# The first 128 tokens of expert 0 gathered from three batches and run through both layers before the gating of the last batch is done

## The chip, the cores and the metric

The kernel runs on one core of one Trainium2 chip. The metric is the device time of one execution in microseconds. A core has a matrix engine (TensorE: PE for its matmuls, PEld for its weight loads), three engines that work on vectors (VectorE or DVE, ScalarE or ACT, GpSimd or POOL) and SyncE (SP), which issues transfers. Each takes its instructions in order; they wait for one another by semaphores. Sixteen DMA engines carry the transfers, which SP, ACT and POOL issue.

## The reference

Causal attention with a decay bias, a mixture of eight experts with one expert per token, and a dense layer with a squared ReLU. Cut to what matters:

```python
# attention: B=4, H=8, S=576, D=64
cum = np.cumsum(np.maximum(s, 0.0), axis=-1)
scores = q @ k.T / np.sqrt(D) + np.minimum(-(cum[:, None] - cum[None, :]), 0.0)   # causal mask
attn_out = softmax(scores) @ v
x = attn_out.transpose(0, 2, 1, 3).reshape(2304, 512)
# mixture: E=8, D=512, F=1024
e_idx = np.argmax(x @ w_gate, axis=1)
gate_w = softmax(x @ w_gate)[arange, e_idx]
eom = sigmoid(x @ w_output_gate)
for e in range(8):
    mask = e_idx == e
    ye = np.maximum(x[mask] @ w1[e], 0.0) @ w2[e]
    out[mask] = gate_w[mask, None] * eom[mask, e, None] * ye
# dense: D=512, F=2048
r = np.maximum(out @ w_in, 0.0)
return (r * r) @ w_out
```

w_in and w_out reach the kernel as 64-bit words, which it converts itself.

## The kernel before

**Attention.** The 32 heads are worked on in 16 pairs, four pairs to a batch of 576 tokens. Scores come from L497, their softmax from DVE (L524) and ACT (L541), the probabilities are transposed on PE (L557) and multiplied by v (L595). The normalised result is transposed back (L633), multiplied by the gate weights (L635), and the token rows are written to a DRAM tensor `x_d`.

**Gating.** When a batch is through, a list of steps `s_lg` to `s_gq` finds each token's expert, its rank among the tokens of that expert (L781 to L785 on PE, L796 and L799 on DVE) and, by one-hot matrices `r` (L804) and small matmuls (`s_tb`, L814), adds to a table of 384 places per expert the number of the token that stands at each place (`tbl`, and `tbl_i` after the last batch, L823). Expert 0's first places are thus known before the last batch, the others only at the end. For the last batch the table is made in three chunks of 128 places, and as soon as a chunk is made, POOL gathers expert 0's rows of it from `x_d` by an indirect DMA (`gather`, L289). While PE has nothing to do in that stretch it runs matmuls on a constant that nobody reads: `warm` (L349, ten and seven) and `warm_h` (L1470, twelve).

**Expert stage.** Expert g has a fixed number of slots, 352 for expert 0, then 320, 304, 304, 288, 288, 272, 256. For precision every fp32 operand is split into a rounded high part and the rest ("hi" and "lo"), and each product takes three passes: hi x hi, lo x hi, hi x lo. The gathered rows are transposed by PE (`x_pe`, L1129), the high part is copied by ACT (`x_hi`, L1135), the low part is made by DVE (`x_lo`, L1140). The hidden layer has eight groups f = 0 to 7, each of 12 matmuls (`emit_h`, L1222), a ReLU on ACT (L1233) and the low part on DVE (L1234), both into one of three buffers of `h_p`; the output layer adds 12 matmuls for each f into four banks (`emit_y`, L1260). A group of h goes into one of four banks, z4 to z7, which the transposes use too (`bank_x`). So an expert takes 96 + 96 matmuls. The result goes to `yT_d`, each expert at the offset that it has in the list of tokens sorted by expert (`y_store`).

**What is loaded beside it.** A pair of halves of the next expert's weights ("a" for the hidden, "b" for the output layer) comes in eight loads of 0.5 MB (`w_load`, L232, on SP into three `stg` buffers and one `stx`), is rounded by ACT (`w_hi`, L241), and its rest is made by DVE (`w_lo`, L245). The 64-bit words of w_in and w_out are converted beside the experts by jobs on DVE, ACT and POOL (L1162 to L1191), whose places start at unit `cv0` and lie `cvp` units apart.

**Between gating and expert 0.** The steps of `perm_steps` count the tokens of every expert (`p_cnt`, L1359), make offsets and a table `tbl_p` of the token numbers of the experts 1 to 7 (DVE, L1364 to L1407), which every later gather needs, and find out whether some expert has more tokens than slots (`p_max`, L1412 on), in which case a loop behind the dense layer works on the rest. SP reads the offsets into registers (`load_regs`). The late gating steps `s_dl` to `s_gq` of batch 3 (`dl` and `zz` on POOL, the exponentials on ACT L855 and L857, the rest on DVE) make the factors by which outputs are multiplied.

**Order.** All of it is emitted as tasks `at(key, fn)`, sorted by key; each engine then works in the order in which its instructions were emitted. A unit of the key is one group f of the expert stage; `te` in the change is the key at which the last pair of heads starts.

Of the kernel before, what the change touches and what calls it, by code (L numbers as in the profile page):

```python
# [12 lines left out]
F32 = mybir.dt.float32  # L13
F32R = mybir.dt.float32r
# [59 lines left out]
    cvp=3.55,  # L74
    cv0=1.2,
# [12 lines left out]
def attention_moe_ffn_kernel(  # L88
# [72 lines left out]
    gap = const.tile([P, 1], F32, name="gap")  # L161
    slot_v = const.tile([1, 3, E], I32, name="slot_v")
# [117 lines left out]

    def gather(g, cs=None):
        if cs is None or cs[0] == 0:
            xr_t[g] = xr_p.tile([P, CH, DM], F32, tag="xr", name="xr")
        t = xr_t[g]
        for c, n in enumerate(rows_of(g)):
            if cs is not None and c not in cs:
                continue
            idx = tbl_i[0:n, c * E:c * E + 1] if g == 0 else tbl_p[0:n, c, g:g + 1]
            nc.gpsimd.indirect_dma_start(  # L289
                out=t[0:n, c, :], out_offset=None, in_=x_d[:, :],  # L290
                in_offset=bass.IndirectOffsetOnAxis(ap=idx, axis=0))
# [11 lines left out]
    with tc.manual_schedule():  # L303
        with ExitStack() as actx:
# [436 lines left out]
            def emit_gate(b, tg, gk):  # L741
# [46 lines left out]

                def s_oid():
# [11 lines left out]
                def s_r1(t, c0=0, c1=CH):  # L801
                    if t == 0 and c0 == 0:
# [70 lines left out]
                steps = [s_lg, s_mx, s_eq, s_cand, s_ix, s_oh, s_pr, s_oid, s_tm, s_rk]  # L873
                if last:
                    ahead = 2
                    for c in range(CH):
                        steps += [partial(s_r1, t, c, c + 1) for t in range(ahead if c else 0, NB)]
                        steps.append(partial(s_tb, c, c + 1))
                        if c + 1 < CH:
                            steps += [partial(s_r1, t, c + 1, c + 2) for t in range(ahead)]  # L880
                        steps += [partial(s_tbl, c, c + 1), partial(gather, 0, [c])]
                else:
                    steps += [partial(s_r1, t) for t in range(NB)] + [s_tb, s_tbl]
                rest = [s_cs, s_ca, s_dl, s_zs, s_pe, s_se, s_rr, s_gq]
                if last:
                    late_steps.extend(rest[2:])
                    steps += rest[0:2]
                else:
                    steps += rest
                for i, st_ in enumerate(steps):  # L890
                    at(tg + (0.001 * i if last else gk[i]), st_)
                if last:
                    at(tg + 0.0055, warm, K_["wm"][3])
                    at(tg + 0.0145, warm, K_["wm"][4])
# [228 lines left out]
        def x_pe(g, c, k0=0, k1=KD):  # L1123
            if c == 0:
                xt_t[g] = xt_p.tile([P, 2, KD, TT], F32R, tag="xt", name="xt")
# [7 lines left out]
        def x_hi(g, c, k0=0, k1=KD):  # L1133
            r = rows_of(g)[c]
            nc.scalar.copy(out=xt_t[g][:, 0, k0:k1, c * P:c * P + r], in_=xp_t[g, c, k0])  # L1135

        def x_lo(g, c, k0=0, k1=KD):
            r = rows_of(g)[c]
            xt = xt_t[g]
            nc.vector.tensor_tensor(  # L1140
                out=xt[:, 1, k0:k1, c * P:c * P + r], in0=xp_t.pop((g, c, k0)),
                in1=xt[:, 0, k0:k1, c * P:c * P + r].bitcast(F32), op=ALU.subtract)
# [71 lines left out]
        def emit_h(g, e, f, fl):  # L1214
            n = sum(rows_of(g))
# [12 lines left out]
        def emit_hv(g, f):  # L1228
            n = sum(rows_of(g))
# [17 lines left out]
        def emit_y(g, e, f, fl, nf, f0=0):  # L1247
# [5 lines left out]
            if g < E:  # L1253
                n = CAPS[g]
# [48 lines left out]
        def emit_yv(g):  # L1303
            ysb = ysb_t[g] = y_p.tile([P, 4, TT], F32, tag="ysb", name="ysb", bufs=1)
            if g < E:
                n = CAPS[g]
# [13 lines left out]
        def y_store(g):  # L1320
            ysb = ysb_t.pop(g)
            if g < E:
                n = CAPS[g]
                dst = yT_d.rearrange("(k p) n -> p k n", p=P)
                nc.sync.dma_start(
                    out=dst[:, :, 0:n] if g == 0 else dst[:, :, ds(reg_o[g], n)], in_=ysb[:, :, 0:n])
# [27 lines left out]
        def perm_steps():  # L1354
# [54 lines left out]
            def p_max():  # L1409
                f = [cnt_f[:, i:i + 1] for i in range(4)]  # L1410
                ov = gt2("ov", [E], 1)
                nc.vector.tensor_tensor(out=ov, in0=R["sv"][:, 2], in1=caps, op=ALU.is_gt)  # L1412
# [54 lines left out]
        def warm_h(n):  # L1467
            wt = bank_x()
            for _ in range(n):
                nc.tensor.matmul(  # L1470
                    wt, lhsT=onesb, rhs=onesb.unsqueeze(1).to_broadcast([P, 512 // P, P]), start=True, stop=True)
# [8 lines left out]
        at(-1.1, warm_h, K_["wm"][5])  # L1480
        for c in range(CH):
            x_trans(0, c, -1.0 + 0.1 * c)
            at(-1.0 + 0.1 * c + 0.0015, warm_h, K_["wm"][6 + c])
        at(0.3, gather, 1)
# [5 lines left out]
        for g in range(E):  # L1490
# [11 lines left out]
            for i, job in enumerate(hj):  # L1502
# [3 lines left out]
                w_job(job, max(ta - K_["wld"], -0.7), ta + K_['wh'], ta + K_['wl'])  # L1506
# [184 lines left out]
```

## Time and profile before

| | |
|---|---|
| time, median of 3 runs | 894.81 us (894.42 to 896.83) |
| time of the profiled execution | 893.0 us |
| its span, first to last instruction | 890.9 us |
| mean granted clock of TensorE | 0.992 |
| busy, share of the span | PE 96%, DVE 58%, ACT 50%, POOL 29% |
| moved by DMA | 121.26 MB, 136 GB/s on average |

A busy share is the time in which an engine works, as a part of the span. The granted clock is given as a part of 2.4 GHz; 0.5 is the lower level of 1.2 GHz. In rows of a timeline the first number is the start in microseconds, the second the time from the start of the row's first instruction to the end of its last, and the number in square brackets the idle time before it and what ended it. The start of the next row on the same engine, less this start, is the row's spacing; matmuls are pipelined, so a row's time is longer than its spacing.

### The profile page before, as it was taken

To read this page: it belongs to the slowest core of one execution; us is meant where nothing else is said; L and a number is where in the kernel's file an instruction comes from. 1 tells how busy PE (TensorE), PEld (TensorE's weight loads), DVE (VectorE), ACT (ScalarE), POOL (GpSimd) and SP (SyncE) were. 2 spreads that over 40 slices of the span, in tenths; PEclk is the share of its full clock that TensorE was granted. 3 is DMA by queue.
4 is the path that set the end of the run, shared out by engine and by line. 5 is a ranking of instruction groups with operands and counts; after the bars stand their busy time and mean duration, and the time that the engine had idled before them with its cause. 6 is when DMAs were issued, how large, how long until landed. Compare 5 with 4: busy or idle time off the path is not lost.

```text
span 890.9 us, 15118 instructions
## 1 busy us (share of the span) xinstructions
PE 854.2 (96%) x5397; PEld 750.0 (84%) x5397; DVE 520.6 (58%) x1180; ACT 448.2 (50%) x997; POOL 261.5 (29%) x299
## 2 busy tenths in 40 slices
PE   7999998899989999999999999999999999999993
PEld 5777776667579999999999888899999999999993
DVE  8777867677666776778766566655333333322221
ACT  6687778788435555655565445444233322322221
POOL 4433144532225455665301232323011011001001
PEclk9999999999999999999999999999999999999997
DMA  6687788886267888988976333221202100000001
GB/s 158 150 192 185 179 198 204 208 189 152 60 207 241 244 232 263 271 263 249 295 228 173 87 119 94 92 86 61 70 36 71 37 37 36 1 1 36 1 0 39
DMA packets 89013, 121.26 MB, mean 136 GB/s; under 512 B 33505, under 2 KB 59105, under 8 KB 88034
## 3 DMA queue, kind: packets, MB, share of 16 engines
q1 hardware_dynamic: 82674, 105.34, 43.7%
q0 software_dynamic: 3664, 9.62, 3.3%
q10 hardware_dynamic: 2592, 5.24, 1.7%
q8 instruction: 45, 0.74, 0.4%
q14 instruction: 38, 0.31, 0.1%
HBM read 80.50 MB, written 23.17 MB: 116 GB/s over the span
## 4 chain that ended last, share of the span: by engine, by line
PE 34%; issue 31%; POOL 9%; ACT 7%; DMA 6%; DVE 6%; SPq 3%; POOLq 0%; ACTq 0%; DVEq 0%
PE z L1260 11%; PE z L1222 11%; PE t L595 3%; PE s L497 3%; POOL cvm L1191 3%; PE t L557 2%; POOL cvm L1190 2%; POOL out_dram L1329 2%; ACT p L541 2%; DMA w_in_d<-cvm 1%; PE z L1129 1%; DVE cvs L1184 1%; DMA xr<-x_d,tbl_p 1%; SPq L448 1%; DMA sta<-aug_d 1%
## 5 line engine op out<-in xcount | busy, mean ns | idle before, releaser
L1222 PE MATMUL z<-xt,w 128*128 128x384 f32 (+6 forms) x1920 | 334.9, 323 | 3.1 <-DVE r L1240 3.0
L1222 PEld LDWEIGHTS z<-xt,w 128*128 128x128 f32 x1920 | 311.6, 188 | 14.1 <-DVE r L1240 6.2
L1269 PE MATMUL z<-w,h 128*128 128x512 f32 x864 | 215.0, 393 | 0.0
L1269 PEld LDWEIGHTS z<-w,h 128*128 128x128 f32 x864 | 160.8, 188 | 29.3
L1240 DVE SCALAR_TENSOR_TENSOR r<-z,r 128x384 f32<-128x384 f32 x96 | 53.3, 555 | 132.4 <-ACT r L1239 131.9
L1260 PE MATMUL z<-h,w 128*128 128x304 f32 (+5 forms) x768 | 115.0, 299 | 0.0
L1239 ACT ACTIVATE r<-z 128x384 f32<-128x384 f32 x96 | 46.8, 488 | 129.2 <-PE z L1222 127.4
L1260 PEld LDWEIGHTS z<-h,w 128*128 128x128 f32 x768 | 108.0, 188 | 0.0
L1190 POOL TENSOR_TENSOR cvm<-cvm,cva 128x512 f32<-128x512 f32 x32 | 43.6, 1361 | 208.5 <-DVE cva L1186 135.7
L1242 ACT CAST h<-r 128x384 fp32r<-128x384 f32 x96 | 49.3, 513 | 85.6 <-DVE r L1240 85.6
L1243 DVE TENSOR_TENSOR h<-r,h 128x384 fp32r<-128x384 f32 x96 | 58.3, 608 | 55.7 <-ACT h L1242 55.7
L1329 POOL DMA_INDIRECT out_dram<-ysb,tok_m x18 | 17.4, 968 | 238.6 <-ACT ysb L1316 176.4
L541 ACT ACTIVATE p<-p,nm 128x128 f32<-128x128 f32 (+3 forms) x144 | 84.4, 591 | 3.9 <-DVE nm L524 3.8
L524 DVE CUSTOM_DVE_ANT_0 p<-s,mask 128x128 f32<-128x128 f32 (+3 forms) x128 | 59.8, 486 | 33.3 <-PE s L497 32.5
L557 PE MATMUL t<-ident,p 128*128 128x128 f32 x400 | 67.4, 281 | 2.2 <-ACT pt L576 0.7
L245 DVE TENSOR_TENSOR w<-stg,w 128x1024 fp32r<-128x1024 f32 x49 | 67.7, 1381 | 0.5 <-ACT w L241 0.4
L557 PEld LDWEIGHTS t<-ident,p 128*128 128x128 f32 x400 | 45.2, 141 | 15.8 <-ACT p L541 8.0
L497 PE MATMUL s<-sta 68*128 68x192 f32 (+7 forms) x204 | 49.8, 340 | 7.9 <-DMA sta<-aug_d 6.7
L1234 DVE SCALAR_TENSOR_TENSOR h<-z,h 128x304 fp32r<-128x304 f32 (+5 forms) x64 | 29.6, 462 | 47.3 <-ACT h L1233 47.1
L241 ACT CAST w<-stg 128x1024 fp32r<-128x1024 f32 x49 | 51.2, 1045 | 8.8 <-DMA stg<-in_moe_w_dram 5.6
L1191 POOL TENSOR_TENSOR cvm<-cvs,cvm 128x512 f32<-128x512 f32 x32 | 54.0, 1686 | 2.5
L595 PE MATMUL t<-pt,v 128*64 128x320 f32 (+4 forms) x448 | 53.1, 368 | 0.0
(223 smaller groups left out, 1016.1 us busy)
## 6 DMA issues: line engine op xcount, KB each, us to landing
stg<-in_moe_w_dram SPq DMA_DIRECT2D x42, 512.0 KB
cv<-in_moe_w_out_dram SPq DMA_DIRECT2D x16, 512.0 KB
stb<-sta SPq DMA_DIRECT2D x14, 576.0 KB
stx<-in_moe_w_dram SPq DMA_DIRECT2D x14, 512.0 KB
cv<-in_moe_w_in_dram SPq DMA_DIRECT2D x14, 512.0 KB
xr<-yT_d SPq DMA_DIRECT2D x8, 768.0 KB
q<-in_q_dram SPq DMA_DIRECT2D x16, 256.0 KB
k<-in_k_dram SPq DMA_DIRECT2D x16, 256.0 KB
```

The costliest lines, as they stand in the source:

```text
L245: nc.vector.tensor_tensor(out=lo, in0=raw.pop(job), in1=hi.bitcast(F32), op=ALU.subtract)
L497: nc.tensor.matmul(ps[0:mw, d0:d0 + nn], lhsT=ql[r, m0:m0 + mw], rhs=kl[r, c0:c0 + nn], start=(i == 0 and (tail or n == 0)), stop=(done an ...
L524: nc.vector.tensor_tensor_reduce(out=dst, in0=src, in1=msk, scale=-1.0, scalar=3.0e38, op0=ALU.add, op1=ALU.min, accum_out=nm[:, c:c + 1])
L541: nc.scalar.activation(out=pt[:, cs], in_=pt[:, cs], func=AF.Exp, scale=-1.0, bias=nm[:, c:c + 1], accum_out=rs[:, r:r + 1])
L557: nc.tensor.transpose(tp[:, i * P:(i + 1) * P], pt[:, j0:j0 + P], ident)
L595: nc.tensor.matmul(o[64 * hd:64 * hd + 64, c0:n], lhsT=vt[r0:P, jb, hd, :], rhs=pt[r0:P, hd, jb, c0:n], start=(jb == 0), stop=(jb == last))
L1190: nc.gpsimd.tensor_tensor(out=m, in0=m, in1=a.bitcast(F32), op=ALU.mult)
L1191: nc.gpsimd.tensor_tensor(out=m, in0=sq, in1=m, op=ALU.add)
L1222: nc.tensor.matmul(ps[:, 0:n], lhsT=wa[:, zw, kk, fl * P:(fl + 1) * P], rhs=xt[:, zx, kk, 0:n], start=(i == 0), stop=(i == 3 * KD - 1))
L1243: nc.vector.tensor_tensor(out=ht[:, 1, 0:n], in0=gg, in1=ht[:, 0, 0:n].bitcast(F32), op=ALU.subtract)
L1260: nc.tensor.matmul(y_acc[g][d][:, 0:n], lhsT=wb[:, zw, fl, d * P:(d + 1) * P], rhs=ht[:, zh, 0:n], start=(f == 0 and i == 0), stop=(f == n ...
L1269: nc.tensor.matmul(acc, lhsT=ht[:, zh, c * P:(c + 1) * P], rhs=wb[:, zw, fl, :], start=(first and i == 0), stop=(last and i == 2))
```

## The change

The first 128 places of expert 0 are taken from the tokens of batches 0 to 2 alone. Batch 2's gating is put three units earlier; then the first chunk of its table is cast (`idx0`) and gathered. In the last pair of heads the rows are transposed and split (`early_xt`, `early_xs`), and `early_h` runs the hidden layer for these 128 tokens, the tokens being the stationary operand and 512 weight columns the moving one: 24 matmuls of 512 columns, 12 of them between the P-V matmuls of the last pair, 9 in the place of the ten warming matmuls, 3 behind the ranks in place of the seven. `early_hr`, `early_ht` and `early_hs` make the ReLU, transpose it and split it, `early_y` runs the output layer in 24 matmuls of 512 columns, `early_yr`, `early_store` and `early_put` copy, transpose and store the result at the head of `yT_d`. Expert 0's stage then runs on the other 224 slots alone. `p_max` has one more comparison: whether batches 0 to 2 held as many tokens of expert 0 as are taken from there. The 12 matmuls of `warm_h` are removed.

```diff
-    cvp=3.55,
-    cv0=1.2,
+    cvp=3.45,
+    cv0=4.0,
...
+    def first_of(g):
+        return 1 if g == 0 else 0
+
+    def cols_of(g):
+        return sum(rows_of(g)) - P * first_of(g)
...
-            idx = tbl_i[0:n, c * E:c * E + 1] if g == 0 else tbl_p[0:n, c, g:g + 1]
+            if g == 0:
+                idx = tbl_i[0:n, c * E:c * E + 1] if c else idx0
+            else:
+                idx = tbl_p[0:n, c, g:g + 1]
...
-                steps = [s_lg, s_mx, s_eq, s_cand, s_ix, s_oh, s_pr, s_oid, s_tm, s_rk]
+                steps = [s_lg, s_mx, s_eq, s_cand, s_ix, s_oh]
                 if last:
+                    steps.append(partial(early_h, 1, 0, 9))
+                steps += [s_pr, s_oid, s_tm, s_rk]
+                if last:
+                    steps += [s_n3, partial(early_ht, 0), partial(early_h, 1, 9, 3 * KD), partial(early_hr, 1)]
+                    steps += [partial(early_hs, 0)]
+                    after = {1: [partial(early_ht, 1)], 2: [partial(early_y, 0, 2)], 0: [partial(early_y, 2, 4)]}
...
+                    steps += [partial(early_hs, 1), partial(early_y, 4, FE // P), early_yr]
...
+                if b == B - 2:
+                    tg -= 3.0
+                    at(tg + gk[16] + 0.05, nc.vector.tensor_copy, idx0, tbl[:, 0:1])
+                    at(tg + gk[16] + 0.06, gather, 0, [0])
...
-                if last:
-                    at(tg + 0.0055, warm, K_["wm"][3])
-                    at(tg + 0.0145, warm, K_["wm"][4])
...
+            def early_hs(half):
+                ps = EA["t", half].rearrange("p (k n) -> p k n", k=4)
+                f = slice(4 * half, 4 * half + 4)
+                nc.scalar.copy(out=hT0[:, 0, f], in_=ps)
+                if half == 0:
+                    raw = early_f32().rearrange("p (k n) -> p k n", k=4)
+                    nc.scalar.copy(out=raw, in_=ps)
+                    nc.gpsimd.tensor_tensor(out=hT0[:, 1, f], in0=raw, in1=hT0[:, 0, f].bitcast(F32), op=ALU.subtract)
+                else:
+                    nc.vector.tensor_tensor(out=hT0[:, 1, f], in0=ps, in1=hT0[:, 0, f].bitcast(F32), op=ALU.subtract)
...
+            def early_yr():
+                nc.scalar.copy(out=xr_t[0][:, 0], in_=EA["y"])
+
+            te = len(K_["order"]) * (NPAIR - 1)
+            at(te + 2.6, early_xt)
+            at(te + 2.7, early_xs)
+            for t, i in ((5.3, 0), (6.04, 3), (6.7, 6), (7.4, 9)):
+                at(te + t, early_h, 0, i, i + 3)
+            at(te + 7.7, early_hr, 0)
...
+        def early_store():
+            ps = bank_x()
+            for kk in range(KD):
+                nc.tensor.transpose(ps[:, kk * P:(kk + 1) * P], xr_t[0][:, 0, kk * P:(kk + 1) * P], ident)
+            t = h_p.tile([P, 2, TT], F32R, tag="h", name="h").rearrange("p a n -> p (a n)")[:, 0:KD * P].bitcast(F32)
+            nc.scalar.copy(out=t, in_=ps)
...
+        def early_put():
+            nc.sync.dma_start(out=yT_d.rearrange("(k p) n -> p k n", p=P)[:, :, 0:P], in_=xp_t.pop("early"))
...
-            at((-0.9 if i < 1 else -0.75) + 0.001 * i, fn)
-        at(-0.74, load_regs, range(1, E), 0, reg_e, E - 1)
+            at(-1.1 + 0.001 * i, fn)
+        at(-1.05, load_regs, range(1, E), 0, reg_e, E - 1)
...
-        at(0.3, gather, 1)
+        x_trans(0, 1, -1.0)
+        x_trans(0, 2, -0.9)
+        at(-0.8, early_store)
+        at(-0.3, early_put)
+        at(-0.6, gather, 1)
...
-                w_job(job, max(ta - K_["wld"], -0.7), ta + K_['wh'], ta + K_['wl'])
+                w_job(job, -0.7 if g == 0 and i < 4 else ta - K_["wld"], ta + K_['wh'], ta + K_['wl'])
```

Where instructions move is seen best in the order of two engines. POOL (GpSimd) from the last batch's one-hot product `oid_all` on, before; `tbl_i` is the index of expert 0's gathers, `tbl_p` that of expert 1's:

```order
L790 TENSOR_TENSOR oid_all<-oh_all,idab 128x80
L289 DMA xr<-x_d,tbl_i 128x512 x2
L289 DMA xr<-x_d,tbl_i 96x512
L845 TENSOR_TENSOR dl<-lgl,mx 128x40
L847 TENSOR_TENSOR zz<-oh_all,lgl 128x40
L870 TENSOR_TENSOR ez<-ez,se 128x5
L871 TENSOR_TENSOR gsq<-ez 128x5
L289 DMA xr<-x_d,tbl_p 128x512 x2
L289 DMA xr<-x_d,tbl_p 64x512
L1190 TENSOR_TENSOR cvm<-cvm,cva 128x512
```

And with the change; the subtract of `early_hs` is L977, and `idx0`'s gather stands further ahead:

```order
L804 TENSOR_TENSOR oid_all<-oh_all,idab 128x80
L977 TENSOR_TENSOR sta_136<-q,sta_136 128x512
L300 DMA xr<-x_d,tbl_i 128x512
L300 DMA xr<-x_d,tbl_i 96x512
L300 DMA xr<-x_d,tbl_p 128x512 x2
L300 DMA xr<-x_d,tbl_p 64x512
L859 TENSOR_TENSOR dl<-lgl,mx 128x40
L861 TENSOR_TENSOR zz<-oh_all,lgl 128x40
L884 TENSOR_TENSOR ez<-ez,se 128x5
L885 TENSOR_TENSOR gsq<-ez 128x5
```

The subtract stands ahead of expert 0's last two gathers, and the three issues of expert 1's gather have moved from behind the late gating steps to ahead of them.

ACT (ScalarE) at the start of expert 0, before (`xt` are the casts of transposed rows, `h` the ReLU of a group):

```order
L1135 CAST xt<-z_3800 128x4x96
L855 ACTIVATE pe<-dl 128x40
L857 ACTIVATE ez<-zs 128x5
L1162 DMA cv<-in_moe_w_in_dram 128x1024
L1233 ACTIVATE h<-z_3934 128x352
```

And with the change, from the copy of the early result on (L1581 is the copy of `early_store` into a buffer of `h_p`):

```order
L992 COPY xr<-s 128x512
L1241 CAST xt<-z_3926 128x4x128
L1241 CAST xt<-z_3933 128x4x96
L1581 COPY h<-z_3940 128x512
L869 ACTIVATE pe<-dl 128x40
L871 ACTIVATE ez<-zs 128x5
L1340 ACTIVATE h<-z_3993 128x224
L1269 DMA cv<-in_moe_w_in_dram 128x1024
L1340 ACTIVATE h<-z_4079 128x224
```

Two copies stand ahead of the exponentials, one of them into a buffer that the ReLUs share, and the first load of the conversion has moved behind the first ReLU.

SP, with the change, once the register loads are through; before, the first two weight loads stood there and no store (`stg` and `stx` are the weights' buffers):

```order
L234 DMA stg<-in_moe_w_dram 128x1024
L234 ISA
L234 DMA stg<-in_moe_w_dram 128x1024
L234 ISA
L234 DMA stg<-in_moe_w_dram 128x1024
L234 ISA
L234 DMA stx<-in_moe_w_dram 128x1024
L1585 DMA yT_d<-h 128x4x128
```

The store of the early result, which empties that `h_p` buffer, is issued behind the four loads.

## Rows read from the trace of the kernel before

**Rows 1.** The page: busy time, share of the span and instructions of each engine.

```profile
PE 854.2 (96%) x5397; PEld 750.0 (84%) x5397; DVE 520.6 (58%) x1180; ACT 448.2 (50%) x997; POOL 261.5 (29%) x299
```

**Rows 2.** Table of stretches: length, then busy us of PE, PEld, DVE, ACT, POOL; clock, DMA share, GB/s.

```profile
210.00:220.00 10.00, 9.81 (x90) 7.66 (x88) 8.13 (x34) 8.50 (x25) 1.96 (x2) 1.00 0.60 157
...
240.00:245.00 5.00, 4.40 (x20) 2.29 (x21) 1.35 (x7) 0.59 (x1) 2.83 (x5) 0.67 0.48 144
...
260.00:265.00 5.00, 2.93 (x20) 2.64 (x19) 1.91 (x3) 1.18 (x2) 0.76 (x1) 1.00 1.03 327
```

**Rows 3.** Timeline of PE, end of attention and gating.

```profile
228.84 0.63 PE L557 MATMUL t<-ident,p 128*128 128x128 f32 x4 [0.68 <-ACT pt L576]
...
234.36 2.32 PE L349 MATMUL t<-onesb 128*128 128x512 bf16 x10
```

**Rows 4.** Timeline of PE, stage of expert 0 and the start of expert 1.

```profile
248.12 6.11 PE L1222 MATMUL z<-xt,w 128*128 128x352 f32 x36
...
256.76 0.63 PE L1129 MATMUL z<-ident,xr 128*128 128x128 f32 x4 [0.61 <-DMA xr<-x_d,tbl_p]
257.14 2.17 PE L1222 MATMUL z<-xt,w 128*128 128x352 f32 x12
...
263.30 0.66 PE L1129 MATMUL z<-ident,xr 128*128 128x128 f32 x4 [2.07 <-DMA xr<-x_d,tbl_p]
...
287.18 1.92 PE L1222 MATMUL z<-xt,w 128*128 128x320 f32 x12
```

**Rows 5.** Timeline of PE, matmuls of 256 columns (expert 7) and of 512 (dense layer).

```profile
454.67 1.60 PE L1260 MATMUL z<-h,w 128*128 128x256 f32 x12
...
466.19 3.04 PE L1260 MATMUL z<-h,w 128*128 128x256 f32 x24
...
573.66 2.24 PE L1269 MATMUL z<-w,h 128*128 128x512 f32 x9
575.74 2.27 PE L1222 MATMUL z<-xt,w 128*128 128x384 f32 x12
```

**Rows 6.** Timeline of DVE, batch 2's gate work, then from the transposed rows to expert 0.

```profile
226.25 1.07 DVE L862 TENSOR_SCALAR ez<-ez 128x5 f32<-128x5 f32 x1
...
246.16 1.16 DVE L1140 TENSOR_TENSOR xt<-z,xt 128x512 fp32r<-128x512 f32 x2 [0.72 <-ACT xt L1135]
247.23 0.16 DVE L1364 COPY ysb<-z 128x8 f32<-128x8 f32 x1
...
250.52 0.18 DVE L1407 CAST tbl_p<-ysb 128x24 int32<-128x24 f32 x1
...
253.77 0.50 DVE L1234 SCALAR_TENSOR_TENSOR h<-z,h 128x352 fp32r<-128x352 f32 x1
```

**Rows 7.** Timelines of DVE and PE where the early gather and its transposes will stand.

```profile
216.54 0.41 DVE L668 TENSOR_TENSOR xs<-s,rca 128x256 f32<-128x256 f32 x1
...
223.16 0.63 PE L690 MATMUL t<-oTx,wp 128*32 128x256 f32 x6
```

**Rows 8.** The gather's line, 235 to 300 us: time from the transfer's issue to landing.

```profile
DMA to landing us min/median/max: 3.3/3.5/8.8
```

**Rows 9.** Timelines of SP and of ACT: the first weights of expert 1.

```profile
254.23 5.50 SPq L232 DMA_DIRECT2D stg<-in_moe_w_dram  x3
...
263.82 1.05 ACT L241 CAST w<-stg 128x1024 fp32r<-128x1024 f32 x1 [3.84 <-DMA stg<-in_moe_w_dram]
...
265.25 0.47 ACT L1233 ACTIVATE h<-z 128x352 fp32r<-128x352 f32 x1
```

**Rows 10.** Timeline of POOL: a subtract of 512 columns, a small one, and expert 1's gather.

```profile
226.01 1.28 POOL L268 TENSOR_TENSOR w<-stg,w 128x512 fp32r<-128x512 f32 x1 [4.57 <-ACT w L264]
...
243.00 0.26 POOL L845 TENSOR_TENSOR dl<-lgl,mx 128x40 f32<-128x40 f32 x1
...
253.12 1.01 POOL L289 DMA_INDIRECT xr<-x_d,tbl_p  x1 [0.59 <-issue]
...
255.69 0.92 POOL L289 DMA_INDIRECT xr<-x_d,tbl_p  x1 [0.30 <-issue]
```

More of the change, by code (lines that the diff above doesn't have):

```diff
@@ L801, in s_r1 @@
                 def s_r1(t, c0=0, c1=CH):
-                    if t == 0 and c0 == 0:
+                    if "r1" not in T:
                         T["r1"] = r1_p.tile([P, NB, CH * P], BF16, tag="r1", name="r1")
@@ new lines, in early_xt, with early_xs, early_h @@
+            def early_xt():
+                ps = EA["x"] = bank("s")
+                for kk in range(KD):
+                    nc.tensor.transpose(ps[:, kk * P:(kk + 1) * P], xr_t[0][:, 0, kk * P:(kk + 1) * P], ident)
+            def early_xs():
+                ps = EA["x"].rearrange("p (k n) -> p k n", k=KD)
+                nc.scalar.copy(out=x0[:, 0], in_=ps)
+                nc.vector.tensor_tensor(out=x0[:, 1], in0=ps, in1=x0[:, 0].bitcast(F32), op=ALU.subtract)
+            def early_h(half, i0, i1):
+                if half == 0 and i0 == 0:
+                    EA["h"] = ps_s.tile([P, 1024], F32, tag="s2", name="s2", bufs=1)
+                wa = half_views((0, "a"))
+                seq = [(zw, zx, kk) for zw, zx in ((0, 0), (1, 0), (0, 1)) for kk in range(KD)]
+                c = slice(512 * half, 512 * half + 512)
+                for i in range(i0, i1):
+                    zw, zx, kk = seq[i]
+                    nc.tensor.matmul(
+                        EA["h"][:, c], lhsT=x0[:, zx, kk], rhs=wa[:, zw, kk, c],
+                        start=(i == 0), stop=(i == 3 * KD - 1))
@@ new lines, in early_hr, with early_ht @@
+            def early_hr(half):
+                c = slice(512 * half, 512 * half + 512)
+                EA["r", half] = early_f32()
+                nc.scalar.activation(out=EA["r", half], in_=EA["h"][:, c], func=AF.Relu)
+            def early_ht(half):
+                ps = EA["t", half] = bank("s")
+                for i in range(4):
+                    nc.tensor.transpose(ps[:, i * P:(i + 1) * P], EA["r", half][:, i * P:(i + 1) * P], ident)
+            def early_hs(half):
[8 more added lines that the diff above has]
+                    nc.vector.tensor_tensor(out=hT0[:, 1, f], in0=ps, in1=hT0[:, 0, f].bitcast(F32), op=ALU.subtract)
@@ new lines, in early_y @@
+            def early_y(f0, f1):
+                if f0 == 0:
+                    EA["y"] = bank("s")
+                wb = half_views((0, "b"))
+                for f in range(f0, f1):
+                    for i, (zh, zw) in enumerate(((0, 0), (0, 1), (1, 0))):
+                        nc.tensor.matmul(
+                            EA["y"], lhsT=hT0[:, zh, f], rhs=wb[:, zw, f, :],
+                            start=(f == 0 and i == 0), stop=(f == FE // P - 1 and i == 2))
+            def early_yr():
+                nc.scalar.copy(out=xr_t[0][:, 0], in_=EA["y"])
@@ L1214, in emit_h @@
         def emit_h(g, e, f, fl):
-            n = sum(rows_of(g))
+            n = cols_of(g)
             xt = xt_t[g]
@@ L1465, in alloc_next @@
             nxt[0] += 1
[L1467 to L1471, printed above, removed]
+        def early_store():
+            ps = bank_x()
+            for kk in range(KD):
+                nc.tensor.transpose(ps[:, kk * P:(kk + 1) * P], xr_t[0][:, 0, kk * P:(kk + 1) * P], ident)
+            t = h_p.tile([P, 2, TT], F32R, tag="h", name="h").rearrange("p a n -> p (a n)")[:, 0:KD * P].bitcast(F32)
+            nc.scalar.copy(out=t, in_=ps)
+            xp_t["early"] = t.rearrange("p (k n) -> p k n", k=KD)
+        def early_put():
+            nc.sync.dma_start(out=yT_d.rearrange("(k p) n -> p k n", p=P)[:, :, 0:P], in_=xp_t.pop("early"))
         first, then = perm_steps()
         for i, fn in enumerate(first):
-            at((-0.9 if i < 1 else -0.75) + 0.001 * i, fn)
-        at(-0.74, load_regs, range(1, E), 0, reg_e, E - 1)
+            at(-1.1 + 0.001 * i, fn)
+        at(-1.05, load_regs, range(1, E), 0, reg_e, E - 1)
         for i, fn in enumerate(late_steps + then):
```

62 lines of the change are left out of this document (41 added, 21 removed).

## The prediction

> **What bounds the kernel now.** Read the page's busy shares first: TensorE (PE) is busy 96% of the span [rows 1], so nearly every microsecond that PE waits or computes counts. The change touches only the end of attention, the gating of batch 3 and the stage of expert 0, so the next view is the table of stretches there [rows 2]: around 240 to 265 us PE is far from full, the granted clock has one fall (0.67 between 240 and 245, that is about 3.3 us at the lower level of 1.2 GHz, since 0.33 x 5 / 0.5 = 3.3), and the DMA engines are full at 260 to 265. The PE timeline says what it does in that time: ten full warming matmuls [rows 3], then the token table, the gather of expert 0, its transposes, and at 248.12 the first h layer [rows 4]. Two waits lie inside the stage, 0.61 and 2.07 us listed, both for the gather of expert 1 [rows 4]. From 265 us on PE runs without a gap. I use one marker, the start of expert 1's third h group, at 287.18 in before [rows 4]: what the change does to that moment, it does to the total, as behind it PE is full in both orders.
>
> **The matmul time saved.** Between 248.12 and 287.18 lie 39.06 us: 192 matmuls of 352 columns, 24 of 320, three sets of transposes (0.4 us each from start to next start) and the waits, 0.77 and 2.22 us counted from start to start. A dozen of 320 columns is listed with 1.92 us [rows 4], of which 0.16 overlaps the next group (as 1.60 listed stands against 1.44 from start to start at 256 columns [rows 5]); so the 24 take 3.5 us, and 31.4 are left, 163 ns a matmul. The new width is 224. The nearest rows are 256 columns: 8 groups of 12 from 454.67 to 466.19, 120 ns each [rows 5]. In proportion to the columns 224 would take 107; I take 112, bounds 107 and 120. Saved: 192 x (163 - 112) = **9.8 us** (8.3 to 10.8).
>
> **The work added in attention.** 4 transposes (0.4) and 12 matmuls of 512 columns now stand among the last pair's P-V matmuls. Such a matmul takes 231 ns: 9 from 573.66 to 575.74 [rows 5]. That is 2.8 + 0.4, and 0.25 us for the ReLU that stands ahead of copies PE waits for. Against it stands an idle of 0.68 us at 228.84 [rows 3] which I expect to vanish: DVE is late there, and 1.07 us of its lateness is batch 2's gate work at 226.25 [rows 6], which the change moves three units earlier. Net **+2.8 us** (2.4 to 3.5). The early gather itself: its table is ready about 216.5 (its neighbour on DVE [rows 7]) and its transposes stand behind the row at 223.16 [rows 7], so it has some 7 us. A lone gather lands in 3.5 us, the slowest took 8.8 [rows 8]. The DMA share there is 0.60 [rows 2], so I cost it at nothing; the other end is 1.5 us.
>
> **The tail of the gating.** On before's clock, without the 2.8: nine h matmuls (2.1 us) fill the place of the ten warming ones (2.32 busy [rows 3]). Three more follow behind the ranks; half 1 is ready at about 238. Then ACT does the ReLU, the rounded copy and the raw copy, about 0.5 us each by its nearest row [rows 9], to 239.7, and POOL's subtract takes 1.28 [rows 10]: 241.0. PE's third y matmul waits for that, an idle of some 1.2 us. The 22 y matmuls behind it and the last table cost 22 x 0.231 + 0.35 = 5.4: 246.5. ACT's copy of y frees p_cnt behind it at 247.3, and DVE's chain, 247.23 to 250.70 in before [rows 6], runs from 247.6 to 251.1. The x_lo pair (1.16 [rows 6]) now stands behind that chain, not ahead of it: 252.2. PE has done 8 matmuls of expert 0's first h group by then, so the group's start stands at 251.3 against 248.12: **+3.2 us**. The two chunk gathers queue behind POOL's subtract and land in 3.5 us by 246.7, hidden.
>
> **Waits inside expert 0.** 28 matmuls after 252.2 end at 255.35. The first y matmuls need h0's low part. Its chain: the three issues of expert 1's gather (3.5 us, 253.12 to 256.61 in before [rows 10]) now stand on POOL ahead of two subtracts (0.26 each [rows 10]), and ACT's exponentials, behind them h0's ReLU, wait for those. From 251.1 that gives 255.1; in before 3.1 us passed from 250.70 to the first h low part [rows 6]; I add 3.3 to the start and 0.5 for the op: 258.9. Eight y matmuls need no low part, so PE waits about **2.6 us**, and y0 ends at 259.3. Transposes, h3, y1, transposes: 262.8. Next is the early store. Its copy sits in one of the three h buffers, so the ReLU of f=2 waits until the store has landed, and h4 on PE waits for that. SP issues it behind seven register loads and four weight loads. In before the first weight load was issued at 254.23 [rows 9]; here 0.4 later, and I let 1.6 us pass until data move, about half of a lone gather's 3.5 [rows 8]: 256.2. 2.1 MB of weights, 0.26 MB of the store and part of one 0.5 MB conversion load at 327 GB/s [rows 2] last to about 264.5. ACT and DVE add 0.8: 265.3, a wait of **2.5 us**. The low end is a store that passes the loads: issued at 257, landed 3.5 later, no wait. The high end is all that is queued by then (with 0.66 MB of gathers and two conversion loads 4.1 MB): 268.6, a wait of 5.8. The before-trace speaks for the middle or worse: the second weight load, issued under 1 us after the first, was used only at 263.82, after 3.84 us of idle ACT [rows 9].
> The Trainium skill, "DMA: Bandwidth & Descriptors", section on queues, rings and completion order, says that descriptors of one issuing engine are consumed in ring order on each DMA engine. By it the store moves after the four loads and the sum stays at -1.7; were the store free to pass, the sum would be -4.2. Those late weights agree with the rule; no row of before has a small transfer behind large ones.
> After 265.3: ten groups of 12 x 0.112, one set of transposes and two groups of expert 1 (1.76 each): 17.3, so 282.6. DVE and ACT must convert expert 1's weights in the shorter stage; I find some 1.4 us of margin and cost it at nothing; gone, it costs what it lacks. The later conversion start (1.2 to 4.0) has the same end and costs nothing while POOL has room.
>
> **The sum.** 282.6 + 2.8 = 285.4 against 287.18: -1.7 us. By terms: -9.8 saved, +2.8 attention, +3.2 tail, +5.1 new waits less 3.0 old ones. The profiled execution took 893.0 us, 1.8 under the median; 891.3 against it, **893.1** against the median of 894.8. (0.3%, 2.7 us, is about what a measurement of this kernel tells from no change.)
>
> **Rivals.** *A, one of the new waits does not appear.* Store early: -4.2. Both covered: 1.7 + 5.1 = -6.8. For: the waits are queueing estimates, and a gather alone lands in 3.5. Against: DMA at 1.03 in that stretch [rows 2]. Time 888.0 to 890.6.
> *B, slower: the clock.* The stage now falls into bursts between waits of 1.2, 2.0, 2.6 and 2.5 us, where before had two. If the clock halves as between 240 and 245 [rows 2], an episode of 3.3 us costs 1.7. One makes it 0.0, two +1.7, three +3.4: 894.8 to 898.2. It decides from the second episode. For: the fall in before came where PE did tiny matmuls and waits. Against: the 2.07 us idle before 263.30 [rows 4] left the clock at 1.00 [rows 2], and here y matmuls of full width stand between the tiny ones.
> The Trainium skill, "TensorE: Matmul & The Clock Gate", part 1 on the clock gate, says that a PE left idle falls to 1.2 GHz; by it these waits are the danger, and the row at 260 to 265 shows one that was not.
> *C, the early gather is late.* It lands after 223.7, PE waits in attention, up to 1.5 us: 893 to 894.5. The slack is small, but the DMA is not full.
> *D, the change doesn't do what it says.* If fewer than 128 tokens of batches 0 to 2 chose expert 0, the new comparison sends the kernel into the overflow loop. With 1728 tokens for 8 experts that is all but excluded.
>
> **How the numbers follow.** Forecast 0.45, with its own range of 891.0 to 896.0 (width 107 to 120: -1.0 to +1.5; attention -0.4 to +0.7; landing -1 to +3). A 0.25, B 0.22, C 0.07, D 0.01. Faster by over 0.3% (below 892.1): all of A and a quarter of the forecast, 0.37. Slower (over 897.5): two thirds of B (three episodes, or two with a landing 1 us late), and a tenth of the forecast, where a landing 3 us late meets one episode: 0.20 with D. Same 0.43. The range reaches from the middle of A to the upper end of B: 888.5 to 898.2.
>
> **What would show it.** In the profile after: expert 0's matmuls at 107 to 120 ns spacing; the first of them near 252 (248.12 + 2.8 + about 1, then a stop after eight); an idle before the first y group ended by DVE's h low part, and a second before the fifth h group, whose chain leads to the early store landing 8 to 10 us after its issue; the idle before 228.84 gone; expert 1's third h group at 285.4. The forecast is wrong if the store lands within 4 us, if POOL's gather issues do not delay the exponentials, or if the granted clock is below 0.8 in two of the 5-us stretches after 245.

## The result and the profile after

The changed kernel takes 908.12 us (median of 4, 905.94 to 910.25) where the kernel before takes 895.82 in the same runs: ratio 1.0132, 95% interval 1.0087 to 1.0177. Slower by 12 us, where 1.7 us less was forecast, and outside the range. The profiled execution has a span of 904.0 us against 890.9, 13.1 us more.

The view that finds the 13 us is the PE timeline of both kernels side by side: the same matmul's start, after less before.

| the same PE instruction | before | after | shift | forecast |
|---|---|---|---|---|
| scores of the last pair, 192 columns | 214.98 | 215.73 | +0.8 | 0 |
| scores of the last pair, 512 columns | 219.09 | 221.83 | +2.7 | 0 |
| first of the ten warming / nine h matmuls | 234.36 | 240.44 | +6.1 | +2.8 |
| first h group of expert 0 (without its stop) | 248.12 | 257.37 | +9.3 | +6.0 |
| marker: third h group of expert 1 | 287.18 | 294.06 | +6.9 | -1.7 |
| expert 4, seventh h group | 386.35 | 396.49 | +10.1 | -1.7 |
| expert 6, first h group | 419.37 | 433.97 | +14.6 | -1.7 |
| end of the span | 890.9 | 904.0 | +13.1 | -1.7 |

257.37 is 258.30 less eight matmuls of about 0.116 us. Between the rows shown the shift is constant to 0.1 us over long stretches (6.88 to 6.89 from 287 to 379 in before). Of the first +0.8, 0.5 stands at 204 us already, in code that the change does not touch; there the shift comes and goes (0.6 at 18 us, 0.05 at 43, 2.1 at 168).

The table of stretches, after and then before (us, then busy time of PE, PEld, DVE, ACT and POOL; granted clock, DMA share, GB/s):

```profile
215.00:240.00 25.00, 22.79 (x179) 15.04 (x176) 14.08 (x51) 14.15 (x41) 6.07 (x10) 1.00 0.18 50
240.00:290.00 50.00, 40.36 (x296) 36.45 (x295) 32.22 (x105) 18.53 (x42) 14.49 (x16) 0.90 0.50 153
...
385.00:430.00 45.00, 40.59 (x287) 39.89 (x286) 30.68 (x45) 23.26 (x41) 25.61 (x22) 0.92 0.85 226
```

```profile
240.00:290.00 50.00, 45.48 (x279) 41.77 (x280) 31.64 (x84) 21.33 (x37) 21.31 (x23) 0.97 0.67 217
...
385.00:430.00 45.00, 45.00 (x349) 44.81 (x348) 32.97 (x46) 27.41 (x48) 27.61 (x27) 1.00 0.87 270
```

Two things stand there. PE is idle for 9.6 us of 240 to 290 (before 4.5) and for 4.4 us of 385 to 430 (before none). And the clock is at its lower level for 10 us of the first stretch ((1 - 0.90) x 50 / 0.5; before 3) and for 7 us of the second (before 0). The timeline of PE, after, where [rows 3, 4] stood, and then in experts 4 and 5:

```profile
221.53 0.55 PE L568 MATMUL t<-ident,p 128*128 128x128 f32 x3 [1.94 <-ACT p L552]
...
231.60 0.63 PE L568 MATMUL t<-ident,p 128*128 128x128 f32 x4 [0.27 <-DVE lw L731]
231.98 0.96 PE L956 MATMUL s<-w,sta 128*128 128x512 f32 x3
...
258.30 5.01 PE L1329 MATMUL z<-xt,w 128*128 128x224 f32 x28 [1.79 <-DVE xt L1247]
263.15 1.05 PE L1367 MATMUL z<-h,w 128*128 128x224 f32 x8
265.61 0.71 PE L1367 MATMUL z<-h,w 128*128 128x224 f32 x4 [1.40 <-DVE h L1341]
...
267.92 1.50 PE L1367 MATMUL z<-h,w 128*128 128x224 f32 x12
269.27 0.60 PE L1234 MATMUL z<-ident,xr 128*128 128x128 f32 x4
274.13 2.90 PE L1329 MATMUL z<-xt,w 128*128 128x224 f32 x12 [4.27 <-DVE h L1341]
276.83 2.56 PE L1367 MATMUL z<-h,w 128*128 128x224 f32 x12
...
391.70 1.57 PE L1329 MATMUL z<-xt,w 128*128 128x288 f32 x5 [1.64 <-DVE h L1341]
...
419.26 3.25 PE L1329 MATMUL z<-xt,w 128*128 128x288 f32 x12 [2.76 <-DVE h L1341]
```

The clock's price can be read here: a dozen of 224 columns takes 1.41 us from start to next start at full clock (266.51 to 267.92; 1.35 from 267.92 to 269.27), and 2.70 behind the idle of 4.27 us (274.13 to 276.83). The granted clock there, by 5 us:

```profile
270.00:275.00 5.00, 0.87 (x4) 0.87 (x5) 1.31 (x2) 1.70 (x4) 0.00 (x0) 0.72 0.33 116
275.00:280.00 5.00, 5.00 (x28) 4.82 (x28) 4.71 (x10) 2.83 (x7) 0.17 (x1) 0.60 0.62 156
```

**The gate of batch 2.** POOL and ACT near 218:

```profile
218.03 1.22 POOL L300 DMA_INDIRECT xr<-x_d,idx  x1 [1.49 <-DVE nm L535]
219.29 0.26 POOL L859 TENSOR_TENSOR dl<-lg,mx 128x40 f32<-128x40 f32 x1
```

```profile
219.58 0.24 ACT L869 ACTIVATE pe<-dl 128x40 f32<-128x40 f32 x1 [0.73 <-POOL dl L859]
...
220.76 0.62 ACT L552 ACTIVATE p<-p,nm 128x384 f32<-128x384 f32 x1
```

The early gather is issued ahead of batch 2's two subtracts; the exponential on ACT waits for them, the softmax of the pair stands behind it, and PE waits 1.94 us for that softmax.

**The early store.** The chain of waits in expert 0:

```profile
263.13 10.08 DMA yT_d<-h
273.25 0.04 issue
273.30 0.37 ACT h L1340
273.69 0.40 DVE h L1341
```

The store lands 10.1 us after its issue; the ReLU of f=2 needs its buffer.

**The conversion.** ACT and DVE before PE's idle at 391.70:

```profile
382.96 0.33 ACTq L1303 DMA_DIRECT2D w_out_d<-cvm  x1
...
389.71 0.67 ACT L1285 ACTIVATE cvm<-cv 128x512 f32<-128x512 uint16 x1 [4.36 <-DMA w_out_d<-cvm]
...
390.75 0.41 ACT L1340 ACTIVATE h<-z 128x288 fp32r<-128x288 f32 x1
```

```profile
391.19 0.46 DVE L1341 SCALAR_TENSOR_TENSOR h<-z,h 128x288 fp32r<-128x288 f32 x1 [3.07 <-ACT h L1340]
```

The conversion has one buffer `cvm`. Its next copy on ACT waits until the store of the job before has landed, 6.7 us after issue here, and a ReLU stands behind that copy. The same happens at 417.75 (4.24 us). Such a wait is not new: ACT's waits from 290 to 500 (total, times, longest), before and then after, are

```profile
ACT cvm L1178 <- DMA w_out_d<-cvm: 9.8, 5, 3.2
```

```profile
ACT cvm L1285 <- DMA w_out_d<-cvm: 13.9, 6, 4.4
```

In before, PE has no idle in that stretch, so none of these waits reaches it there.

### The profile page after: what moved, and what is told of

The parts are those of the page before. It is cut to its first block, busy times and chain, and to the rows that moved or that the text cites. A ratio compares the mean times of both kernels' runs of the same rounds, so it can differ in the third digit from the quotient of the medians.

```text
span 904.0 us, 15200 instructions
## 1 busy us (share of the span) xinstructions
PE 860.1 (95%) x5428; PEld 757.5 (84%) x5428; DVE 519.7 (57%) x1183; ACT 452.3 (50%) x1005; POOL 269.4 (30%) x300
## 4 chain that ended last, share of the span: by engine, by line
PE 36%; issue 31%; POOL 8%; DMA 7%; ACT 7%; DVE 6%; SPq 2%; POOLq 0%; ACTq 0%; DVEq 0%
PE z L1329 11%; PE z L1367 10%; PE s L508 4%; PE t L606 4%; PE t L568 3%; POOL cvm L1298 2%; DMA w_out_d<-cvm 2%; POOL cvm L1297 2%; POOL out_dram L1436 2%; ACT p L552 2%; DMA sta<-aug_d 1%; SPq L459 1%; PE t L422 1%; DMA yT_d<-h 1%; DMA w_in_d<-cvm 1%
## 5 line engine op out<-in xcount | busy, mean ns | idle before, releaser
L1367 PE MATMUL z<-h,w 128*128 128x304 f32 (+5 forms) x768 | 111.9, 295 | 1.4 <-DVE h L1341 1.4
L1367 PEld LDWEIGHTS z<-h,w 128*128 128x128 f32 x768 | 105.5, 191 | 1.6 <-DVE h L1341 1.6
L508 PE MATMUL s<-sta 68*128 68x192 f32 (+7 forms) x204 | 52.0, 352 | 6.5 <-DMA sta<-aug_d 5.2
L1298 POOL TENSOR_TENSOR cvm<-cvs,cvm 128x512 f32<-128x512 f32 x32 | 56.1, 1754 | 2.5
```

The lines of the kernel that those rows point to most:

```text
L508: nc.tensor.matmul(ps[0:mw, d0:d0 + nn], lhsT=ql[r, m0:m0 + mw], rhs=kl[r, c0:c0 + nn], start=(i == 0 and (tail or n == 0)), stop=(done an ...
L1298: nc.gpsimd.tensor_tensor(out=m, in0=sq, in1=m, op=ALU.add)
L1367: nc.tensor.matmul(y_acc[g][d][:, 0:n], lhsT=wb[:, zw, fl, d * P:(d + 1) * P], rhs=ht[:, zh, 0:n], start=(f == 0 and i == 0), stop=(f == n ...
```

## The experiments

The theory: three faults that the forecast missed or undersized (the order on POOL at batch 2's gate, the store's buffer, the conversion's places), each followed by some time at the lower clock. The rivals are in each run's text. The ratios are against the kernel before. Each trace is one execution.

### The conversion's places: cv_old, before_cv_new, step_old

```diff
# cv_old: the changed kernel with
-    cvp=3.45,
-    cv0=4.0,
+    cvp=3.55,
+    cv0=1.2,
# before_cv_new: the kernel before with 3.45 and 4.0
# step_old: the changed kernel with cvp=3.55 alone
```

> The changed kernel with the conversion's places as they were (start 1.2, step 3.55). Theory, places: the two PE idles inside experts 3 and 4 (1.64 and 2.76 us, each ended by a low part of h that stands behind a copy waiting for the conversion's store) come from the new places; they go, with the clock falls behind them, and the time drops by 5 to 8 us against the changed kernel, to a ratio near 1.006. But the first conversion then shares the transfers of expert 0's stage again, so the early store may land later. Rival, later experts: the idles come from the experts being 7 us late against the table writes; then they stay or move, and the time stays within 2 us of the changed kernel.

Measured: 902.38 us, ratio 1.0074 (1.0052 to 1.0095). (The expectation speaks of experts 3 and 4; by the index used elsewhere here they are 4 and 5.) PE has no idle from 290 to 500, and the shift stays at 11.4 us from expert 1 to expert 7. Where the changed kernel lost 4.4 us and 7 us at the lower clock, the table of stretches of cv_old shows

```profile
385.00:430.00 45.00, 45.00 (x346) 44.60 (x346) 34.80 (x48) 27.64 (x48) 24.93 (x22) 1.00 0.83 263
```

The rival is refuted: the experts are later there than in the changed kernel and have no idle. The first conversions share expert 0's transfers again, as expected; there PE waits 4.35 us. That wait leads not to the early store but to the conversion's own load, for which ACT waits with a ReLU behind it:

```profile
274.54 0.68 ACT L1281 ACTIVATE cvs<-cv 128x512 f32<-128x512 f32 x1 [8.29 <-DMA cv<-in_moe_w_in_dram]
```

> The kernel before with only the conversion's places of the change (start 4.0, step 3.45). Theory, places: idles of 1 to 3 us appear in experts 3 to 5 of the kernel before too, ratio 1.003 to 1.008. Rival, the places matter only together with the late experts: ratio 1.000.

Measured: 896.8 us, ratio 1.0026 (0.9999 to 1.0053). The idles do appear in the kernel before, as its waits of PE from 290 to 500 show (total, times, longest):

```profile
PE z L1222 <- DVE h L1234: 2.5, 2, 1.5
```

But its idle of 2.07 us in expert 0 [rows 4] is gone, as the first conversion's loads no longer stand beside expert 1's gather: the marker comes 2.3 us earlier by the shift from 257 to 264, and 2.8 us are lost at 383 and 407. So the new places do hurt without the rest, and give something too; the sum is near zero there.

> The changed kernel with the conversion's step as it was (3.55) and its new start (4.0). Theory, step: a job's copy follows the store of the job before by 1.15 units with the new step and 1.25 with the old; the lost 0.1 unit (0.35 us) and the place it has among the weights make ACT wait 4.3 us; with the old step the two idles near 391 and 417 get shorter by no more than 0.4 each if only the distance counts. Rival, phase: the place of the stores among the weight loads and gathers counts, which both start and step set; then the idles move to other experts or go.

Measured: 906.8 us, ratio 1.0146 (1.0122 to 1.0169). The idles move: 3.16 us at 314.10, 0.60 at 427, 1.86 at 452. That is the rival, phase: the distance to the store before is not what decides, but where the jobs fall among the loads of weights and gathers. No run with the old start and step together has an idle of PE from 290 to 500.

### The order at batch 2's gate: gate_order, gate_back

```diff
# gate_order
-                    at(tg + gk[16] + 0.06, gather, 0, [0])
+                    at(tg + gk[19] + 0.01, gather, 0, [0])
# gate_back: the changed kernel with
-                    tg -= 3.0
-            at(te + 2.6, early_xt)
+            at(te + 3.3, early_xt)
-            at(te + 2.7, early_xs)
+            at(te + 3.4, early_xs)
```

> The changed kernel with the early gather of chunk 0 put behind the two subtracts of batch 2's gating on POOL. Theory: the gather's issue (1.2 us) held back the subtracts, ACT's exponential and, behind that, the softmax for which PE idled 1.94 us near 220; that idle goes and the time drops by 1.5 to 2.2 us. Rival, the gate of batch 2 is simply too early (three units): the idle stays at 1 us or more.

Measured: 902.82 us, ratio 1.0090 (1.0065 to 1.0116). The idle falls from 1.94 to 1.02 us: 0.9 was the gather's issue, 1.0 stays, so both theories had half. That the time fell by more comes from later: the store's wait is 2.04 us there, the idles in the experts are 3.25 us, and no stretch from 290 to 600 has a lower clock.

> The changed kernel with batch 2's gating left where it was, the early gather behind it, and the transposes of its rows 0.7 unit later. Theory: the idle near 220 (1.94 us, 1.02 with the gather behind the subtracts) comes from the gate work being squeezed into the softmax of that pair; left where it was, the idle is under 0.5 us, an idle of up to 0.7 us near 229 comes back, and the gather still lands in time: 1 to 2 us less than the changed kernel. Rival, late gather: PE waits at the transposes (about 228) and the time is the same or worse.

Measured: 901.25 us, ratio 1.0089 (1.0056 to 1.0123). The idle near 220 is gone, 0.81 and 0.33 us stand near 229.5 and 230.5, and the gather is in time. The last scores of attention stand as they did against the marks ahead of them (shift 0.69 at 203.85 and 0.70 at 226.40 in before, where the changed kernel goes from 0.51 to 3.18, 0.44 of it for the early transposes, which stand behind that mark here). So the move of the gate cost 2.2 us up to that mark and brought back 0.9 behind it (one idle of 0.27 us there in the changed kernel): net 1.3 us by the end of the last P-V matmuls.

### The early store: own_buffer, store_first

```diff
# own_buffer: the free end of the table's scratch tile
-            t = h_p.tile([P, 2, TT], F32R, tag="h", name="h").rearrange("p a n -> p (a n)")[:, 0:KD * P].bitcast(F32)
+            t = scr["t"][:, 1024:1024 + KD * P]
# store_first
-        at(-0.3, early_put)
+        at(-0.75, early_put)
```

> The changed kernel with the early store read from the free end of the table's scratch tile, not from one of the three h buffers. Theory: the fourth h group waited only for the store's landing (10.1 us after issue); PE's idle of 4.27 us at 274 goes and with it the fall of the clock behind it (2.6 us): 4 to 7 us less than the changed kernel. Rival, the weights' transfers or their rounding on ACT and DVE are late there in any case: an idle of 2 us or more stays in that place and the time drops by under 3 us.

Measured: 902.54 us, ratio 1.0079 (1.0057 to 1.0101). The idle of 4.27 us is gone; in PE's timeline the group that waited follows its transposes at once:

```profile
271.60 0.60 PE L1234 MATMUL z<-ident,xr 128*128 128x128 f32 x4
271.96 1.58 PE L1329 MATMUL z<-xt,w 128*128 128x224 f32 x12
```

From the ninth matmul of the first h group (258.30 in the changed kernel) to the marker this kernel gains 8.8 us on the kernel before, its shift goes from 11.2 to 2.4; the changed kernel gains 2.0 there. The forecast had 7.7 from the group's start, some 7.3 from that matmul, with 2.5 of the store's wait in it.

> The changed kernel with the early store issued on SP ahead of the four weight loads, its buffer shared as before. Theory, queue: the store took 10.1 us because 2 MB of weights stood ahead of it; ahead of them it lands 3 to 5 us after its issue, PE's idle of 4.27 us before the fourth h group shrinks to under 1 us, and the time drops by 3 to 6 us against the changed kernel, as with a buffer of its own. Rival, shared engines: it moves beside all that is in flight wherever it stands, lands after 7 us or more, and an idle of 2 us or more stays.

Measured: 900.16 us, ratio 1.0069 (1.0045 to 1.0094). No ReLU waits for the store any more. The store's issue in SP's timeline:

```profile
262.56 0.39 SPq L1585 DMA_DIRECT2D yT_d<-h  x1
```

The last update of its semaphore in this trace stands at 266.07, 3.5 us after the issue, as the theory said; behind the four loads it was 10.1. It was the queue. PE still idles 1.84 us in that place, now at the end of another transfer in the chain of waits, the first weights, issued 0.95 us behind the store:

```profile
263.51 7.59 DMA stg<-in_moe_w_dram
```

So the rival's number came true (an idle near 2 us) by another cause than its own: what is behind in the queue is now the weights. From the ninth matmul of the first h group to the marker this kernel gains 5.1 us on the kernel before, the changed kernel 2.0 and own_buffer 8.8; the rest of the lower time lies in the experts, whose idles (3.5 us) are followed by no lower clock.

### The late gating steps: late_steps_first

```diff
-        at(-0.6, gather, 1)
+        at(-0.495, gather, 1)
```

> The changed kernel with expert 1's gather put behind the two late subtracts on POOL. Theory: the wait of PE for the first low part of h (1.40 us near 265) goes, since ACT's exponentials no longer wait for three gather issues; but the store's wait stands right behind it and takes the gain, so that the time is within 1.5 us of the changed kernel. Rival, the chain on DVE sets that wait: the idle of 1.4 stays.

Measured: 902.66 us, ratio 1.0095 (1.0064 to 1.0126). The idle of 1.40 is gone and the store's idle grows from 4.27 to 4.52. The shift at the marker is 6.35 against 6.88: half a microsecond, as expected; the rest of the lower time lies in the experts, as in gate_order.

### Together: all_four, all_gate_back, all_four_xlo_first, all_four_warm

all_four has the edits of cv_old, gate_order, own_buffer and late_steps_first. all_gate_back adds gate_back's. all_four_xlo_first adds to all_four, beside moving `early_store` to -0.5985 and the first weight loads to -0.54, so that their order stays,

```diff
-            at(-1.1 + 0.001 * i, fn)
-        at(-1.05, load_regs, range(1, E), 0, reg_e, E - 1)
+            at((-1.1 if i < 1 else -0.6) + 0.001 * i, fn)
+        at(-0.55, load_regs, range(1, E), 0, reg_e, E - 1)
```

and all_four_warm adds `at(-0.04, warm_h, 8)`.

> The changed kernel with all four: the conversion's old places, the early gather behind batch 2's subtracts, the early store out of its own buffer, expert 1's gather behind the late subtracts. Theory: the terms add: 5 to 6 for the conversion with its clock falls, 1 for the gate, 4 to 7 for the store, 1 for the late steps, so 893 to 898 where the kernel before takes 896, ratio 0.997 to 1.003. Rival, each removed wait turns into a later one: ratio 1.005 or more.

Measured: 891.32 us (median of 10), ratio 0.9958 (0.9942 to 0.9974): faster than the kernel before, by 0.4%, and than the changed kernel by 1.7%. The four single ratios lie 0.0058, 0.0042, 0.0053 and 0.0037 under 1.0132, together 0.0190; all four give 0.0174. That is near, but it does not show that four separate terms add: the intervals are about as wide as the single differences, and by stage the runs overlap. Growth of the shift in us:

| | from 204 us to the ninth matmul of the first h group | from there to the marker | from the marker to 500 us |
|---|---|---|---|
| changed kernel | +8.4 | -2.0 | +7.6 |
| cv_old | +10.0 | -0.6 | -0.1 |
| gate_order | +7.4 | -3.3 | +3.5 |
| own_buffer | +11.4 | -8.8 | +8.7 |
| late_steps_first | +9.8 | -4.1 | +3.8 |
| all_four | +7.3 | -9.2 | -0.1 |

gate_order and late_steps_first owe most of their gain to the last column, which cv_old empties altogether. cv_old, own_buffer and late_steps_first lose 1.4 to 3.0 us against the changed kernel in the first column, which their edits hardly touch; each has time at the lower clock there. What is shown is that the four together remove the loss. Its stretches:

```profile
240.00:290.00 50.00, 44.97 (x355) 40.97 (x356) 36.08 (x111) 24.99 (x55) 19.97 (x20) 0.97 0.59 192
...
385.00:430.00 45.00, 45.00 (x347) 44.81 (x347) 33.77 (x46) 26.80 (x45) 28.06 (x27) 1.00 0.84 262
```

Idle and clock are those of before, with 355 matmuls, many of them narrower, in place of 279 in the first stretch.

> As all_four, with batch 2's gating left where it was and the transposes of the early rows 0.7 unit later. Theory: another 0.5 to 1.5 us less than all_four, ratio 0.995 to 1.002. Rival, late gather: equal or worse.

Measured: 891.78 us, ratio 0.9955 (0.9937 to 0.9973): no difference from all_four.

> all_four, and the low part of the transposed rows ahead of the offset table's chain on DVE, as in the kernel before. Theory: PE's idle of 1.79 us inside the first h group goes; the table, the register loads, the weights and expert 1's gather come 1.2 us later, so that 0.5 to 1.5 us remain: ratio 0.994 to 0.997. Rival, the delay comes back at the transposes of expert 1 (idle 1.08 us in all_four): same as all_four.

Measured: 897.62 us, ratio 1.0040 (1.0020 to 1.0061): worse than either theory. The idle of 1.79 inside the first group is 1.34 ahead of it now, and the delay comes back larger: 4.93 us of idle at 277.69, whose chain leads to expert 1's first weights, issued behind the later registers:

```profile
268.01 7.05 DMA stg<-in_moe_w_dram
```

So the table's chain is rightly ahead of the low parts; that part of the change pays for itself.

> all_four, and eight of the removed constant matmuls put back ahead of the first h group, where PE waits 0.4 and then 1.8 us. Theory, clock: the wait costs twice, by itself and by the lower clock behind it (3.0 us at half in all_four, 1.5 us lost); the eight take 1.73 us out of the 2.2, so the clock stays up and 0 to 1.5 us are gained. Rival, the clock falls whatever PE does there, or the eight delay the group: 0 to 1 us lost.

Measured: 892.63 us (median of 12), ratio 0.9987 (0.9970 to 1.0004). The clock does stay up, as its stretch shows, but PE idles 1.22 us ahead of the first h group and 1.73 ahead of the fourth, where all_four has 0.41, 1.79 and 1.08:

```profile
240.00:290.00 50.00, 45.22 (x365) 40.41 (x362) 36.74 (x112) 24.70 (x55) 20.07 (x20) 1.00 0.59 192
```

In the profiles the marker's shift is 0.67 against 1.35 in all_four, but 0.46 of that stands at 204 us already, and the time is not better. Not settled by these runs; the changed kernel itself was not run with these matmuls.

## Why the prediction was wrong

Point by point, by its own terms:

- **Matmul time saved: right.** 1.35 us a dozen is 112 ns a matmul, the value taken.
- **Work added in attention: right in size.** From 221.83 to 240.44 the shift grows by 3.3, which is 0.5 for the transposes and 3.3 for the twelve (2.8 forecast, and 0.25 for the ReLU), less 0.4 of the idle at 228.84; +2.8 was forecast, with 3.5 as its upper end. The idle did not vanish, 0.27 us of it stays. The early gather was in time, rival C did not occur, nor D.
- **Moving batch 2's gate, costed at nothing: failed.** The step counted the gather's landing and its issue not at all, though it is an instruction of POOL with two subtracts behind it, and behind these ACT's softmax. Its idle cost 1.9 us: 0.9 for the issue (gate_order), 1.0 for the gate work in that place (gate_back).
- **Tail: right.** +3.2 forecast, 9.25 - 6.08 = 3.17 measured, with the idles it named, though not of its sizes: 0.86 at the third y matmul (1.2 forecast), 0.67 at p_cnt, 1.79 for the low parts. (Its 246.5 should be 246.4, 241.0 + 5.4.) That the sum fits to 0.03 is luck.
- **Waits in expert 0: right in place and cause, undersized in one.** The wait for the low part is 1.40 us instead of 2.6, but not because the low part was early: from the ninth matmul of the first h group to the end of y0 pass 7.9 us where 7.1 were forecast. PE itself came later, as it was at the lower clock (granted 0.86 from 255 to 260, 0.80 from 260 to 265). From there to the end of the store's wait pass 8.0 us where 6.0 were forecast (an idle of 4.27 instead of 2.5): the store landed 10.1 us after its issue, where the sum has some 7.5, from an issue at 257 to 264.5, and the prediction's sign 8 to 10 (own_buffer, store_first). The high end of that term, 268.6, leaves out the 0.8 for ACT and DVE that the middle has. The Trainium skill's rule on ring order (DMA: Bandwidth & Descriptors, section "Queues, rings and completion order") agrees: ahead of the loads the store landed in 3.5 us and held nobody up. From there to the marker pass 19.9 us where 17.3 were forecast; 2.4 of that is the clock.
- **The clock: a rival, and it came.** B asked for two episodes; 10 us at the lower level stand in 240 to 290, against 3 before, and 7 more in 385 to 430, some 3.3 us of PE time there. By the rows of expert 0, 28 matmuls from 258.30 take 4.85 us and 24 from 274.13 take 5.20, some 1.7 and 2.4 more than at full clock; the first stands ahead of the wait for the low part and is mostly hidden in it (argued from the rows: the low part hangs on POOL's issues and not on PE). The prediction's own sign of being wrong came too, a granted clock below 0.8 in two stretches of 5 us: 0.72 and 0.60 from 270 to 280. The forecast's sum gave the clock no term at all, though it had itself added four waits. What cannot be shown here is when a wait brings the fall: in the changed kernel 1.64 us at 392 did (the stretch from 390 to 395 has 0.67), in gate_order's profile 1.96 us at 389 did not.
- **The conversion's later start "costs nothing while POOL has room": failed, the largest miss.** 7.7 us in the changed kernel's profile (14.60 - 6.88), 4.4 of idle and 3.3 of clock; some 1.8 come back at the dense layer, where before had waits of its own. POOL had room (25.6 us busy of 45); what had none was the single buffer and the store that must leave it. cv_old has none of this loss. The new step of 3.45 got no term at all. With this fell the premise of the marker, that "behind it PE is full in both orders": from 290 to 500 us it is in before and is not in the changed kernel.

The span was missed by 14.8 us (13.1 slower, 1.7 faster forecast). By the shifts: 7.7 from the conversion's places, 2.0 from the moved gate, 5.4 in expert 0 (2.0 from the end of y0 to the end of the store's wait, 2.4 of clock behind it, 1.0 in small differences), 0.5 in the twelve matmuls, 0.8 that stood ahead of all this, less some 1.5 that come back by the end. So the terms of expert 0 summed to a gain, as own_buffer and all_four show, and the loss came from two moved pieces that were costed at nothing, from a store costed too low and from the clock behind the waits.

## What to carry to other kernels

Cost a moved step by what is behind it on every queue that it enters, its DMA issue as well: here 1.2 us on POOL reached PE over two engines as 0.9. A job with a single buffer that is emptied by a store has a due time of its own in each place; when its place is changed, look through the whole stretch for the wait of its next copy, not only through the part that was meant. A wait of PE can cost more than its length: behind the idle of 1.64 us here another 1.5 were lost at the lower clock. And a shorter total does not prove the cause that an edit was meant for: read by stage where the time fell.

## What was not expected of the hardware

Whether a wait was followed by the lower clock differs between kernels whose code is the same there: gate_order and late_steps_first have 3.3 and 3.6 us of idle in experts 4 and 5 and no fall, the changed kernel and own_buffer 4.4 and 4.5 us and 7 us at the lower level. These are single profiles, so it is not shown what decides it. Also in attention, from 120 to 200 us, the profiles have 0 to 14 us at the lower clock, from kernel to kernel, and shifts of up to some 4 us; single profiles should be compared stage by stage and not by their spans.
